# Splitting most gate and up weights in the prologue, turning the row maxima through DRAM, and asking for shared weight loads in an attention and GLU block

## The chip, the cores and the metric

The kernel runs on one core of a Trainium2 chip. The metric is the device time of one execution in microseconds (us). Three runs of the kernel before the change took 1661.74, 1663.04 and 1664.35 us, with a median of 1663.04. One more execution was taken with the hardware profiler; it took 1663.57 us, and its span from the first to the last instruction is 1661.8 us.

## What is computed

One transformer block over 2048 tokens of width 512, with a modulation vector computed from `c`. Attention has 32 query heads of width 16 and one shared key and value head; the feed-forward has a hidden width of 1792 and a sigmoid gate.

```
mod = silu(c) @ w_mod                      # six rows of 512: sa, ca, ga, sb, cb, gb
h = layernorm(x) * (1 + ca) + sa
q, k, v = h @ wq, h @ wk, h @ wv           # q: 32 heads x 16; k, v: one head x 16
p = softmax(q k^T / 4)                     # over all 2048 keys
x = x + ga * ((p v) @ wo)
h = layernorm(x) * (1 + cb) + sb
x = x + gb * ((sigmoid(h @ w_gate) * (h @ w_up)) @ w_down)
```

## The kernel before, in words

**Numbers as pairs.** Large products run in 16-bit floats, with every operand split into a high part and a low remainder, so that a product is three passes (high by high, high by low, low by high). The products for `p v` run in 32-bit floats.

**Units and steps.** Attention is cut into 32 units: 16 blocks of 128 queries (`QU`), each in two halves of 16 heads. A unit has 16 steps (`NKB`), one for 128 keys each, so the main loop (L1190) has 512 steps. A step has two half-steps. In each half-step, in the order that `ORDER` (L57) writes down, TensorE makes two `a` tiles (scores in one layout, bank `sa`, of which VectorE takes the row maximum into `mx`, L640), two `s` tiles (scores in the other layout, bank `st`, which ScalarE turns into `P` with an exponential, L678) and one `c` group (`P` times `V` into the bank `craw`, L691). The `a` tiles run 84 tiles (`A0`) ahead of the `s` tiles, since the maxima of a unit must be known before its first `s` tile. There are three `sa` banks and two `st` banks (L87). Matmuls are cut into tiles of 64 rows by 32 columns (`columns`, L152), so that the two halves of the array run different things at once: `a` and `s` on one half, `c` on the other.

**The way of the maxima.** When 64 maxima tiles of unit i are there (some five steps before the unit's first step), `max_end` (L652) reduces them with two VectorE instructions, `max_rows` (L659) turns them with two small TensorE matmuls through an `sa` bank, ScalarE copies and scales them twice, VectorE makes the low part, and four DMAs put two rows into each half of the unit's query tile `qp` (rows 48 and 49, 112 and 113). The first `s` tile of the unit reads these rows.

**The feed-forward as filling.** After each block of 128 queries its output projection and feed-forward (`ffn_block`, L868) are handed out in small pieces: `piece` (L1178) puts a few of its matmuls behind each half-step, at a rate that `pace` (L1141) works out from what is left. Pieces are `po` (output projection, group `wo`), `pgu` (gate and up), `pd` (down), and in the first three units `pq` (the queries that the prologue left). A group starts when its inputs are marked as issued a number of steps ago (`needs`: `EGAP` steps for the first block, `HGAP` for the others). The chain ahead of a block's `wo` is `unit_end`, `place`, `recip`, `recip2`, `recip3`, `finish` (L712 to L763): ScalarE evicts `craw` into `cs`, and five dependent steps of DMA, VectorE and GpSimd put the normalized rows into `a`. Behind `wo` come `norm` and `norm2` (L912, L918) on GpSimd with one VectorE statistic between, and a transposing DMA `h<-rows`. `defer(n, f)` means that f is written n steps later.

**The weights.** Gate and up weights, `wo` and the down weights are split into high and low in the main loop by 46 jobs (`weight_jobs`, L808). A job loads 128 by 512 numbers (`wst`), and three GpSimd instructions split them (L370 to L372); gate and up are then stored to DRAM (`wD`) and read again for each block as `gw` tiles. `WSTEPS` = 60 spreads the jobs over 60 steps. The first `gw` load is asked for when the last gate and up job has been stored.

**Queues.** TensorE, VectorE and ScalarE instructions and the DMAs of the main loop (`sp1`, issued by SyncE, SP) stay in written order. GpSimd (POOL) instructions of the main loop are placed by the framework's scheduler. Each queue runs in order, so a DMA that waits for its source holds up the DMAs behind it.

**Prologue.** `PLAN` (L38) is a list of tokens that fixes the order before the main loop: layer norm and transposes of the input (`S`, `N`, `T`, `H`, `E`, `L`), keys and values (`pk`, `KB`, `KL`, `pv`, `V`), the first queries (`q`, `QA`, `QL`), the modulation (`lm`, `pm`, `me`, `pr`, `m`), the first 84 maxima tiles (`a` a product, `x` its maximum), and the maxima chain of unit 0 (`mx`, `my`, `mz`).

Of the kernel before, what the change touches and what calls it, by code (L numbers as in the profile page):

```python
# [56 lines left out]
ORDER = "a0", "s0", "c", "a1", "s1"  # L57
# [5 lines left out]
SKIP = 9  # L63
GAP = 2
EGAP = 4
HGAP = 3
CHAIN = 24
QRATE = 1.5
MOST = 3
# [3 lines left out]
WSTEPS = 60  # L73
WLAST = 66
# [18 lines left out]
NGW = 4 * NPR + 2  # L93


@with_exitstack
def adaln_mqa_glu_kernel(
# [100 lines left out]
    class Couple:  # L198
# [3 lines left out]
        def part(self, n0, n1):  # L202
# [4 lines left out]
            for n in range(n0, n1):  # L207
# [3 lines left out]
                for j in (1 - side[0], side[0]):  # L211
                    g = self.gs[j ^ (n >= m)]
                    l_, r_, *cut = g.term(n % m, slice(64 * j, 64 * j + 64))
                    columns(cut[0](g.bank) if cut else g.bank, l_, r_, n == 0, n == 2 * m - 1)
# [15 lines left out]
    class Halves:  # L230
# [6 lines left out]
        def part(self, n0, n1):  # L237
# [4 lines left out]
            for n in range(n0, n1):  # L242
                for j in (1 - side[0], side[0]):
                    columns(self.banks[j], *self.term(n, slice(64 * j, 64 * j + 64)), n == 0, n == self.n - 1)
                if n in self.after:
                    self.after[n]()
# [36 lines left out]
    xall = pro.tile([P, NKB, D], F32, name="xall")  # L283
# [3 lines left out]
    def load_x(b):  # L287
        sp.dma_start(xall[:, 4 * b:4 * b + 4, :], x[b * QB:(b + 1) * QB, :].rearrange("(t p) d -> p t d", p=P))
# [15 lines left out]
    for t in range(4):  # L304
        sp.dma_start(xall[:, t, :], x[t * P:(t + 1) * P, :])
# [145 lines left out]
    def xs(b):  # L451
        return [xall[:, 4 * b + t, :] for t in range(4)]
# [150 lines left out]
    def load_q(i):  # L603
        b, o = units[i]
        qp = blanks.pop(0) if blanks else blank(pool)
        for j in range(2):
            src = qD[:, 2 * o * P:2 * (o + 1) * P, b * QU:(b + 1) * QU].rearrange("h (r j d) q -> j h d r q", j=2, d=DH)[j]
            for g, hl in ((0, 0), (1, 1), (2, 0)):
                spq().dma_start(qp[64 * j + 16 * g:64 * j + 16 * (g + 1)], src[hl])
        qps[i] = qp  # L610
# [13 lines left out]
    def spot(n):  # L624
        return n // 16, n % 2, n // 2 % 8

    def a_product(i, n):
# [3 lines left out]
        kc, j, r = spot(n)  # L631
# [4 lines left out]
        else:  # L636
            columns(sa, l_, r_, True, True)
        return i, n, sa

    def a_max(i, n, sa):  # L640
        kc, j, r = spot(n)
# [5 lines left out]
    def a_tile(i, n):  # L647
        a_max(*a_product(i, n))
# [3 lines left out]
    def max_end(i):  # L652
        m16 = wp.tile([64, 32], F32, tag="m16", name="m16", bufs=4)
        for u in range(2):
            dve.tensor_reduce(m16.rearrange("p (h u) -> p h u", u=2)[:, :, u], mxs[i][64 * u:64 * u + 64],
                              axis=AX.X, op=ALU.max)
        return lambda: max_rows(i, m16)

    def max_rows(i, m16):  # L659
        qp = get_q(i)  # L660
        pm = sbank("sa")
        pe.matmul(pm[:32, :64], m16, ident[:64, :64], start=True, stop=True)
        m32 = wp.tile([32, 64], F32, tag="m32", name="m32", bufs=4)
        act.activation(m32, pm[:32, :64], AF.Identity, scale=1.0 / SM)
        mh = wp.tile([32, 2, 64], F16, tag="mh", name="mh", bufs=4)
        act.activation(mh[:, 0], m32, AF.Identity)

        def low():
            dve.tensor_tensor(mh[:, 1], m32, mh[:, 0], op=ALU.subtract)
            for h in range(2):  # L670
                for j in range(2):
                    r = 64 * j + 48 + h
                    sp1.dma_start(qp[r:r + 1], mh[16 * j:16 * j + 16, h, :])

        return low
# [51 lines left out]
    def place(b, o, cs, lD, rD):  # L727
# [7 lines left out]
        defer(W1, lambda: recip(b, o, lD, rD))  # L735

    def recip(b, o, lD, rD):
# [11 lines left out]
        def recip3():  # L749
            for z in range(2):  # L750
                sp1.dma_start(raw[:, (2 + z) * QU:(3 + z) * QU], lD[1][8 * z:8 * z + 8].unsqueeze(1).to_broadcast([8, DH, QU]))
            defer(W3, lambda: finish(b, o, raw))

        defer(W2, recip2)
# [566 lines left out]
```

## Time and profile before

| what | us |
|---|---|
| median of three runs | 1663.04 |
| the profiled execution, whole | 1663.57 |
| its span, first to last instruction | 1661.8 |
| prologue, to the first eviction of an `st` bank | 114.8 |
| 32 units, first to last `st` eviction | 1471.0 |
| what follows | 76.0 |

The 1.8 us between the profiled execution's time and its span lie outside the instructions. The page gives for each engine its busy time; matmuls overlap, so a busy TensorE is not one at its peak. A view by stretches gives the busy time of each engine between two times; a unit shows in it as 64 evictions `P<-st`. A timeline gives the start of merged instructions in us from the span's start, then how long the row lasts; what stands in brackets is the idle time ahead of it and what ended it.

### The profile page before, as it was taken

The page shows a single profiled execution, that of the slowest core. Times are in us where ns is not written, and L with a number is a line of the kernel's source. Part 1 is how long each engine was busy: PE and PEld are TensorE (multiplying, and loading weights), DVE is VectorE, ACT ScalarE, POOL GpSimd, SP SyncE. Part 2 cuts the span into 40 slices and gives each one's busy share as a digit, 9 for nine tenths or more (in the row PEclk, how much of TensorE's full clock was granted, in tenths as well). Part 3 has the DMA queues.
Part 4 walks back from the last instruction along what each step waited for, and adds up shares of the span by engine and source line. Part 5 has one row for each costly group of instructions (what it writes and reads, how often), then busy time and mean ns, then how long its engine had stood idle before and what let it go on. Part 6 is the DMA issues. An engine that isn't in the chain of part 4 may idle for free.

```text
span 1661.8 us, 92905 instructions
## 1 busy us (share of the span) xinstructions
PE 1601.6 (96%) x41875; PEld 989.8 (60%) x41875; DVE 1440.8 (87%) x2410; ACT 1302.8 (78%) x2346; POOL 710.2 (43%) x864
## 2 busy tenths in 40 slices
PE   6899997989999999999999999999999999999998
PEld 3335553646666666666666666666666666666544
DVE  7689997879999999999999999999999999998031
ACT  5528886878888888888888888888888888888821
POOL 4353887461442525352534425262525344251510
PEclk9879998999999999999999999999999999999999
DMA  6232555550573535454462735463454537353653
GB/s 211 94 106 74 163 149 163 169 138 21 139 164 85 140 87 127 99 129 114 117 135 86 165 89 142 91 133 82 132 111 120 135 83 165 85 139 88 157 168 107
DMA packets 246681, 203.60 MB, mean 123 GB/s; under 512 B 125468, under 2 KB 177420, under 8 KB 246284
## 3 DMA queue, kind: packets, MB, share of 16 engines
q1 hardware_dynamic: 246284, 197.66, 46.3%
q8 instruction: 328, 5.37, 1.4%
q14 instruction: 69, 0.57, 0.1%
HBM read 159.97 MB, written 20.30 MB: 108 GB/s over the span
## 4 chain that ended last, share of the span: by engine, by line
PE 87%; ACT 4%; DVE 3%; POOL 2%; issue 2%; DMA 1%; SPq 0%; ACTq 0%; POOLq 0%; DVEq 0%
PE craw L143 23%; PE pgu L143 18%; PE sa L143 17%; PE st L143 10%; PE pd L143 8%; PE pq L143 3%; PE po L143 2%; DVE mx L143 2%; PE pd L257 2%; PE pgu L194 2%; ACT P L143 2%; ACT th L143 1%; PE pk L143 1%; DMA wm<-in_w_mod_dram 0%; PE pmod L143 0%
## 5 line engine op out<-in xcount | busy, mean ns | idle before, releaser
L143 DVE TENSOR_REDUCE mx<-sa 128x1 f32<-128x512 f32 x2048 | 1300.9, 683 | 96.7 <-PE sa L143 41.5
L143 ACT ACTIVATE P<-st 128x512 f32<-128x512 f32 x2048 | 1183.6, 597 | 230.2 <-PE st L143 162.6
L143 PE MATMUL craw<-P,V 64*32 64x512 f32 x8192 | 1100.5, 599 | 1.8 <-issue 1.3
L143 PE MATMUL st<-qp,kp 64*32 64x512 f16 x8192 | 844.3, 380 | 11.2 <-ACT P L143 9.7
L143 PE MATMUL sa<-kp,qp 64*32 64x512 f16 (+1 forms) x7940 | 840.7, 380 | 13.5 <-DVE mx L143 10.2
L143 PEld LDWEIGHTS <-kp 64*32 64x32 f16 x8192 | 323.9, 91 | 250.0 <-issue 83.0
L143 PE MATMUL pgu<-gw,h 64*32 64x512 f16 x9600 | 423.9, 377 | 9.3 <-DMA h<-rows 5.0
L143 PEld LDWEIGHTS <-qp 64*32 64x32 f16 (+1 forms) x7940 | 276.1, 92 | 146.1 <-issue 62.5
L143 PEld LDWEIGHTS <-h 64*32 64x32 f16 (+1 forms) x9792 | 209.2, 92 | 90.4 <-issue 28.1
L143 PEld LDWEIGHTS craw<-P,V 64*32 64x32 f32 x8192 | 195.6, 105 | 26.9 <-issue 13.2
L143 PE MATMUL pd<-wdh,g 64*32 64x512 f16 x2912 | 152.7, 376 | 2.4 <-issue 1.5
L967 POOL TENSOR_SCALAR th<-th 128x512 f32<-128x512 f32 (+1 forms) x57 | 32.3, 566 | 254.3 <-ACT th L143 243.6
L143 PEld LDWEIGHTS <-g 64*32 64x32 f16 x4368 | 94.7, 92 | 34.2 <-issue 8.0
L143 PE MATMUL pd<-wdl,g 64*32 64x512 f16 x1456 | 91.0, 376 | 0.0
L1020 POOL TENSOR_TENSOR o<-o,gb 128x512 f32<-128x512 f32 x13 | 16.7, 1282 | 166.1 <-ACT o L143 166.1
L600 POOL MEMSET qp<- 32x1024 f16 x60 | 56.6, 944 | 68.4 <-PE st L143 60.6
L968 POOL TENSOR_TENSOR th<-th,u 128x512 f32<-128x512 f32 (+1 forms) x57 | 65.3, 1146 | 4.8
L895 POOL TENSOR_TENSOR rows<-th,rows 128x512 f16<-128x512 f32 (+1 forms) x57 | 59.5, 1044 | 4.8
L143 PE MATMUL po<-woh,a 64*32 64x512 f16 x960 | 52.9, 377 | 1.9 <-ACT th L143 1.4
L143 PE MATMUL craw<-nought 64*32 64x1 f16 x329 | 53.7, 163 | 0.0
L143 PE MATMUL pq<-h,wdh 64*32 64x512 f16 (+1 forms) x688 | 51.9, 386 | 0.6 <-POOL h L143 0.4
L143 DVE COPY u<-pgu 128x512 f32<-128x512 f32 x43 | 29.3, 681 | 26.1 <-PE pgu L143 26.1
(163 smaller groups left out, 1139.8 us busy)
## 6 DMA issues: line engine op xcount, KB each, us to landing
gw<-wD SPq DMA_DIRECT2D x448, 256.0 KB
wD<-gw SPq DMA_DIRECT2D x28, 256.0 KB
wm<-in_w_mod_dram SPq DMA_DIRECT2D x6, 1024.0 KB
qp<-qD SPq DMA_DIRECT2D x192, 32.0 KB
qD<-q SPq DMA_DIRECT2D x16, 256.0 KB
xr<-in_A_x_dram SPq DMA_DIRECT2D x16, 256.0 KB
out_dram<-ot SPq DMA_DIRECT2D x16, 256.0 KB
rD<-cs SPq DMA_DIRECT2D x124, 32.0 KB
```

What stands on the lines that cost most here:

```text
L143: return (lambda *a, **k: keep(f_(*a, **k))) if pinned else f_
L194: pe.matmul(cut[0](self.bank) if cut else self.bank, l_, r_, start=(n == 0), stop=(n == self.n - 1))
L257: pe.matmul(self.bank, *self.term(n, slice(0, P)), start=(n == 0), stop=(n == self.n - 1))
L600: eng.memset(qp[j:j + 32], 0.0)
L895: pool.tensor_tensor(rows[:, n:2 * n], src, rows[:, :n], op=ALU.subtract)
L967: pool.tensor_scalar(th, th, 1.0, 1.0, op0=ALU.add, op1=ALU.mult)
L968: pool.tensor_tensor(th, th, u_, op=ALU.mult)
L1020: pool.tensor_tensor(o2, o2, mods[5], op=ALU.mult)
```

## The change

It has four parts.

1. **Prologue.** The gate and up weights of five of seven column blocks (`JCH` = 5: 20 jobs) are split in the prologue: ScalarE makes the high part and the scaled copy, GpSimd the low part, each job with one load and two stores by DMA (`jl`, `jb`). The input blocks `xall` become four separate buffers, and two of them are used again by these jobs. 26 jobs are left for the main loop, over 52 steps. `PLAN` is written anew: the query products of the second to fourth group stand later, and the first query tile is loaded in two parts (`la`, `lb`).
2. **First block.** `wo` of block 0 is due after 5 steps of its unit in place of 9, its chain `place` to `finish` has waits of 1 step in place of 2, 3 and 2, `EGAP` is 3 in place of 4, and queries left wait for an urgent group that is due within 7 steps. `last_end` waits 2 steps in place of 1 before ScalarE reads what GpSimd adds.
3. **Maxima.** The chain of the maxima has no matmul: one VectorE reduction, one ScalarE copy, a VectorE difference, a VectorE 32 by 32 transpose, one DMA to DRAM (`mD`) and two DMAs from there into `qp`.
4. **Order and weight loads.** `ORDER` is `s0 a0 c a1 s1`; `spot` gives two `a` tiles that follow each other the same query weights; the second of them, and every third product of a feed-forward group, is written as a matmul that uses weights loaded before (`held`).

```diff
-    'lw0 lw1 lx2 lx3 lw2 lw3 pm1 S00 S01 me1 S02 pr1 S03 ra0 rb0 m1 pm0 rc0 N00 N01 N02 me0 N03 pr0 S10 wh0 S11 wl0 '
+    'lw0 lx2 lx3 lw1 lw2 lw3 pm1 S00 S01 me1 S02 pr1 S03 ra0 rb0 m1 pm0 rc0 N00 N01 N02 me0 N03 pr0 S10 wh0 S11 wl0 '
...
-ORDER = "a0", "s0", "c", "a1", "s1"
+ORDER = "s0", "a0", "c", "a1", "s1"
-SKIP = 9
+SKIP, SKIP0 = 9, 5
-EGAP = 4
+EGAP = 3
+QWAIT = 7
-WSTEPS = 60
-WLAST = 66
+WSTEPS = 52
+WLAST = 52
+JCH = 5
...
-    def columns(dst, l_, r_, start, stop):
+    def columns(dst, l_, r_, start, stop, held=None):
         for c_ in range(0, P, 32):
-            pe.matmul(dst[c_:c_ + 32], l_[:, c_:c_ + 32], r_, start=start, stop=stop)
+            if held is None:
+                pe.matmul(dst[c_:c_ + 32], l_[:, c_:c_ + 32], r_, start=start, stop=stop)
+            else:
+                pe.add_instruction(mybir.InstMatmult(
+                    start_tensor_calc=start, stop_tensor_calc=stop, tile_size=(64, 32), tile_position=(held, c_), ldweights=False,
...
-    def spot(n):
-        return n // 16, n % 2, n // 2 % 8
+    def spot(i, n):
+        if i == 0:
+            return n // 16, n % 2, n // 2 % 8
+        return n // 32 * 2 + n // 2 % 2, n % 2, n // 4 % 8
...
     def max_end(i):
-        m16 = wp.tile([64, 32], F32, tag="m16", name="m16", bufs=4)
-        for u in range(2):
-            dve.tensor_reduce(m16.rearrange("p (h u) -> p h u", u=2)[:, :, u], mxs[i][64 * u:64 * u + 64],
-                              axis=AX.X, op=ALU.max)
...
+        dve.tensor_reduce(m, mxs[i], axis=AX.X, op=ALU.max)
+        return lambda: max_high(i, m, mm)
...
+        act.activation(mm[:, :16], m, AF.Identity, scale=1.0 / SM)
...
+        dve.scalar_tensor_tensor(mm[:, 16:], m, 1.0 / SM, mm[:, :16], op0=ALU.mult, op1=ALU.subtract)
+        dve.transpose(mt, mm)
...
+        sp1.dma_start(mD.rearrange("c (b q) -> b c q", b=4), mt)
+        return lambda: lambda: max_rows(i, mD)
...
+            sp1.dma_start(qp[r:r + 2].rearrange("h r q -> h (r q)"), mD.rearrange("(h j r) q -> j h (r q)", h=2, j=2)[j])
...
-        defer(W1, lambda: recip(b, o, lD, rD))
+        defer(W1 if b else 1, lambda: recip(b, o, lD, rD))
...
-                defer(1, go)
+                defer(2, go)
...
+    def job_beat():
+        k, beat[0] = beat[0], beat[0] + 1
+        if k < len(jobs):
+            w_ = wst["f"][:, k % 4]
+            hi, lo = (wst["h"][:, k % 4, e].rearrange("p k n -> p (k n)") for e in range(2))
+            act.activation(hi, w_, AF.Identity, scale=SW)
+            act.activation(w_, w_, AF.Identity, scale=SW)
+            pool1.tensor_tensor(lo, w_, hi, op=ALU.subtract)
+        if k >= 2:
+            job_store(k - 2)
+            if k + 2 < len(jobs):
+                job_load(k + 2)
...
-            first_.ready = i * NKB + SKIP
+            first_.ready = i * NKB + (SKIP if b > 1 else SKIP0)
```

The built program shows what becomes of part 4 on TensorE. In a half-step in the middle of the main loop (`sa` is an `a` tile, `st` an `s` tile, `craw` the `c` group; the rows left out repeat the pair of rows above them for the other three column tiles) there stood before:

```order
L143 LDWEIGHTS qp
L143 MATMUL sa<-kp,qp 32x512
...
L143 LDWEIGHTS kp
L143 MATMUL st<-qp,kp 32x512
...
L143 MATMUL craw<-P_22350,V 32x512
L143 MATMUL craw<-P_22368,V 32x512
```

And there stands now:

```order
L146 LDWEIGHTS qp
L146 MATMUL sa<-kp,qp 32x512
...
L146 MATMUL craw<-P_22217,V 32x512
L146 MATMUL craw<-P_22240,V 32x512
...
L146 LDWEIGHTS qp
L146 MATMUL sa<-kp,qp 32x512
...
L146 LDWEIGHTS kp
L146 MATMUL st<-qp,kp 32x512
```

The `c` group now lies between the two `a` tiles and no `s` tile does; but the second `a` tile, written as one without a load, has its LDWEIGHTS in the built program all the same. Counted over the whole program there are 33,430 of these rows where there were 33,423, so no weight load has gone.

On the SP queue, in unit 2 (steps 34 to 37), on the way of block 0 to its output projection (`lD`, `rD`, `lc`, `raw` are its stations; `qp<-qD` loads the queries of unit 4) there stood before:

```order
L143 DMA lD<-cs 8x1x128 x2
L143 DMA rD<-cs 16x4x128 x4
L143 DMA wst<-in_B_w_gate_dram 128x2x256
L143 DMA lc<-lD 128x16
L143 DMA wst<-in_B_w_up_dram 128x2x256
L143 DMA qp<-qD 16x8x128 x6
L143 DMA wD<-gw 512x1x256 x2
L143 DMA wst<-in_B_w_gate_dram 128x2x256
L143 DMA lD<-rc 128x16
L143 DMA raw<-rD 128x2x128
```

And now:

```order
L146 DMA lD<-cs 8x1x128 x2
L146 DMA rD<-cs 16x4x128 x4
L146 DMA gw<-wD 128x1024 x2
L146 DMA wst<-in_B_w_down_dram 128x512
L146 DMA lc<-lD 128x16
L146 DMA gw<-wD 128x1024 x2
L146 DMA lD<-rc 128x16
L146 DMA raw<-rD 128x2x128
L146 DMA gw<-wD 128x1024 x2
L146 DMA wst<-in_B_w_down_dram 128x512
L146 DMA qp<-qD 16x8x128 x6
L146 DMA raw<-lD 128x1x128 x2
```

The loads of `gw`, which stood in unit 3, now lie between the stations, and `raw<-lD` comes right behind the six loads of the query tile. A little further on the same queue, ahead of the start of unit 3 (steps 40 to 46), there stood before the rows of the maxima (`qp<-mh`) among loads and stores of weights:

```order
L143 DMA wD<-gw 512x1x256 x2
L143 DMA wst<-in_B_w_gate_dram 128x2x256
L143 DMA wst<-in_B_w_up_dram 128x2x256
L143 DMA qp<-mh 1x16x64 x4
L143 DMA wD<-gw 512x1x256 x2
```

And now:

```order
L146 DMA qD<-q_4459 128x2x512
L146 DMA gw<-wD 128x1024 x2
L146 DMA wst<-in_B_w_down_dram 128x512 x2
L146 DMA_TRANSPOSE h_4963<-rows 128x4x128 x2
L146 DMA mD<-mt 4x32x32
L146 DMA qp<-mD 2x1024 x2
```

The two transposing DMAs of block 0, which wait for GpSimd's `rows`, have come ahead of the two steps of the maxima of unit 3.

More of the change, by code (lines that the diff above doesn't have):

```diff
@@ L282, in adaln_mqa_glu_kernel @@
     cT = cp.tile([P, NDC], F32, name="cT")
-    xall = pro.tile([P, NKB, D], F32, name="xall")
+    xall = [pro.tile([P, 4, D], F32, tag="xb", name="xb", bufs=4) for _ in range(4)]
     wkv = cp.tile([P, 2, NDC, DH], F32, name="wkv")
@@ L451, in xs @@
     def xs(b):
-        return [xall[:, 4 * b + t, :] for t in range(4)]
+        return [xall[b][:, t, :] for t in range(4)]
     pts = {}
@@ L826, in gate_up @@
                          g_[:, :, m], g_[:, :, 2 + m], [2, 256], store if m == 1 else None)
-        for i in range(NCH):
+        for i in range(JCH, NCH):
             for kk in range(2):
@@ L1083, in adaln_mqa_glu_kernel @@
         stages[name](*[int(z) for z in tok[len(name):]])
-    assert not held and apos == A0
+    assert not held and apos == A0 and beat[0] == len(jobs) + 2
     first.clear()
@@ L1106, in adaln_mqa_glu_kernel @@
     early = [Couple(q_group(*z), q_group(*y)) for z, y in zip(qleft[::2], qleft[1::2])]
+    for g in early:
+        g.b = 0
     work, urgent = early, []
@@ L1137, in pick @@
         for z in range(min(2, len(work))):
+            if work[z].stage == "q" and urgent and s > urgent[0].ready - QWAIT:
+                return
             if ready(s, work[z]) and (z == 0 or "dn" in (work[0].stage, work[1].stage)):
@@ L1208, in adaln_mqa_glu_kernel @@
                 z[1]()
-            ready_rows, rows[:] = rows[:], [max_end(*z) for z in late]
             an = A0 + 4 * (s - kb % 2)
```

98 lines of the change are left out of this document (54 added, 44 removed), and 21 rows, old and new, of the table PLAN.

## The prediction

> **What bounds the kernel now.** I read the stretches first, then a half-step in the timeline, the groups, and the waits one by one. The stretches are the prologue (0 to 114.8 us, in two), units 0 and 1, unit 3, units 4 to 9, and units 10 to 31; unit 2 lies between 203.1 and 247.1.
>
> ```profile
> core 0: us, PE busy (x) PEld busy (x) DVE busy (x) ACT busy (x) POOL busy (x), PEclk, DMA share, GB/s
> 0.00:66.00 66.00, 48.22 (x246) 24.15 (x246) 46.80 (x104) 39.34 (x62) 31.29 (x55) 0.90 0.56 191
> 66.00:114.80 48.80, 44.87 (x301) 13.51 (x304) 40.17 (x68) 9.37 (x17) 21.36 (x26) 0.82 0.26 76
> 114.80:203.10 88.30, 85.58 (x2180) 47.28 (x2180) 81.86 (x136) 76.27 (x139) 49.21 (x62) 0.96 0.38 107
> ...
> 247.10:302.60 55.50, 46.44 (x1017) 23.56 (x1012) 42.65 (x72) 37.00 (x69) 41.09 (x51) 0.88 0.55 172
> 302.60:584.70 282.10, 273.17 (x7771) 175.73 (x7755) 260.88 (x433) 233.98 (x423) 121.57 (x146) 0.99 0.47 119
> 584.70:1585.80 1001.10, 991.47 (x28903) 649.82 (x28894) 907.50 (x1498) 858.55 (x1549) 405.91 (x478) 1.00 0.49 118
> ```
>
> TensorE is the bound wherever the filling is full. Units 10 to 31 take 1001.1/22 = 45.5 us each, 1.422 per half-step; units 0 and 1, with little filling, take 88.3/64 = 1.38. Unit 3 takes 55.5: ten too many. What a half-step holds is in the timeline of TensorE:
>
> ```profile
> 947.37 2.53 DVE L143 TENSOR_REDUCE mx<-sa 128x1 f32<-128x512 f32 x4
> 947.97 0.40 PE L143 MATMUL sa<-kp,qp 64*32 64x512 f16 x4
> 948.19 0.40 PE L143 MATMUL st<-qp,kp 64*32 64x512 f16 x4
> ...
> 948.62 0.40 PE L143 MATMUL st<-qp,kp 64*32 64x512 f16 x4
> 948.83 0.49 PE L143 MATMUL pd<-wdl,g 64*32 64x512 f16 x8
> ```
>
> A maximum's tile and an `s` tile start 0.215 us apart (two pairs in 0.43), weight loads included, and the terms of the feed-forward behind them too. Four tiles and two terms of the feed-forward make 6 x 0.215 = 1.29; the `c` group runs on the other half. VectorE needs 2.53/4 = 0.63 per maximum. ScalarE's price, and how often TensorE is empty because of the two, stand in the groups:
>
> ```profile
> L143 ACT ACTIVATE P<-st 128x512 f32<-128x512 f32 x2048 | 1183.6, 597 | 230.2 <-PE st L143 162.6 <-PE sa L143 8.3 <-PE pgu L143 2.3
> L143 PE MATMUL st<-qp,kp 64*32 64x512 f16 x8192 | 844.3, 380 | 11.2 <-ACT P L143 9.7 <-issue 1.2
> L143 PE MATMUL sa<-kp,qp 64*32 64x512 f16 x7856 | 813.1, 379 | 5.0 <-DVE mx L143 4.6
> ```
>
> The long stops are single ones:
>
> ```profile
> 263.53 0.61 PE L143 MATMUL sa<-kp,qp 64*32 64x512 f16 x4 [3.71 <-DVE mx L143]
> 285.63 0.63 PE L143 MATMUL pgu<-gw,h 64*32 64x512 f16 x8 [4.30 <-DMA h<-rows]
> 367.96 0.62 PE L143 MATMUL st<-qp,kp 64*32 64x512 f16 x4 [5.31 <-ACT P L143]
> ```
>
> The first two lie in unit 3. VectorE's wait behind the first is for GpSimd, which was splitting weights between two instructions of `norm`:
>
> ```profile
> 257.41 1.27 POOL L914 TENSOR_TENSOR xr<-t,xr 128x512 f32<-128x512 f32 x1
> ...
> 260.00 0.62 POOL L370 TENSOR_SCALAR wst<-wst 128x512 f32<-128x512 f32 x1
> ...
> 283.09 1.15 POOL L895 TENSOR_TENSOR rows<-t,rows 128x512 f16<-128x512 f32 x1
> ```
>
> **The change part by part**, against the profiled execution's 1663.57 us, which is 0.5 above the median of the runs.
>
> *Weight loads.* Not one goes (the count in the built program), and rows 0.215 apart show them hidden anyway: 0.
>
> *Prologue.* Twenty jobs add two ScalarE instructions and one GpSimd instruction each; nearest rows:
>
> ```profile
> L143 ACT ACTIVATE wdh<-wqs 128x512 f16<-128x512 f32 x4 | 2.5, 630 | 1.0 <-DMA wqs<-in_A_wq_dram 1.0
> L143 POOL TENSOR_TENSOR wdl<-wqs,wdh 128x512 f16<-128x512 f32 x3 | 3.5, 1155 | 3.7 <-ACT wqs L143 3.7
> ```
>
> ScalarE: 20 x 2 x 0.63 = 25.2 us on the 9.4 busy of 48.8. GpSimd: 20 x 1.16 = 23.2 on 21.4, 44.6 of 48.8. DMA: 256 KB in and 256 KB out per job, 10.5 MB; at the 191 GB/s that cost a share of 0.56 in the first 66 us that is 10.5/(0.191/0.56) = 31 us of the 48.8 x 0.74 = 36 free. VectorE, 40.2 of 48.8 and the bound there with its 84 maxima, gets nothing. So 0, with GpSimd's near-full stretch as the cover; if the jobs wait for each other, +6; if query products put later relieve it, -4.
>
> *Units 0 to 2, spacing.* Here ScalarE binds: 2 x 0.597 = 1.19 of 1.38. The `s` tiles stood 0.43 and 0.95 apart; `a0` between them makes it 0.65 and 0.73. I take a third of the 0.19 for 64 half-steps, -4 (-10 to +3).
>
> *Unit 2, block 0 comes early.* A new stop. SP's queue in unit 2 before:
>
> ```profile
> 208.16 1.17 SPq L143 DMA_DIRECT2D lD<-cs  x2
> 209.37 1.79 SPq L143 DMA_DIRECT2D rD<-cs  x4
> 211.21 0.43 SPq L143 DMA_DIRECT2D wst<-in_B_w_gate_dram  x1
> 211.75 1.27 SPq L143 DMA_DIRECT2D lc<-lD  x1
> 213.06 0.44 SPq L143 DMA_DIRECT2D wst<-in_B_w_up_dram  x1
> 213.54 3.90 SPq L143 DMA_DIRECT2D qp<-qD  x6
> ```
>
> Landing, the price of two `gw`, and GpSimd's share are in these, of unit 3:
>
> ```profile
> 285.76 1.33 SPq L143 DMA_DIRECT2D raw<-lD  x2
> ...
> 287.14 0.92 SPq L143 DMA_DIRECT2D gw<-wD  x2
> ```
>
> ```profile
> 288.90 0.73 POOL L760 TENSOR_TENSOR raw<-raw 128x256 f32<-128x256 f32 x1 [4.66 <-DMA raw<-lD]
> 289.72 0.41 POOL L761 TENSOR_SCALAR a<-raw 128x256 f16<-128x256 f32 x1
> ```
>
> Now, from the same 208.16: `lD` 1.17, `rD` 1.79, two `gw` 0.92, a load 0.44, `lc` 1.27 and two `gw` 0.92 end at 214.7. Then `lD<-rc` and `raw<-rD` (as long as a load and as `lc`'s shortest, some 0.4 each), two `gw`, a load, the six `qp<-qD` (3.90) and two `raw<-lD` (1.33): 222.1, or 223 if the reciprocal is waited for. GpSimd starts 288.90 - 287.09 = 1.8 us behind that and takes 0.73 + 0.41 for the high part of `a`: 225 to 226, with a low part of some 0.7 behind it. The group `wo` is due at step 38.5, at 203.1 + 6.5 x 2.75 = 221.0, and is urgent, so TensorE stops for 4 to 6 us. The `norm` steps that follow put a VectorE statistic behind GpSimd again, 1 to 2 us. I take +7 (+2 to +12).
>
> *Unit 3.* Both stops and the shortage of filling go: the feed-forward starts nine steps earlier, and unit 3 gets 504 of its matmuls where it had 224 (counted in the built program, as all such counts here). GpSimd's chain from 257.41 to 284.24, 26.8 us, held five splits of 0.62 + 0.62 + 1.16 = 2.4 us; in the changed order two stand there. What takes the place of the stops: `mD` for unit 3 stands on SP behind the transposes `h<-rows`, which wait for that chain. I take it 4 us late (0 to 7). So 55.5 becomes 45.2 + 4 = 49.2: -6.3.
>
> *Units 4 to 9.* 282.1 us; at 45.5 each they would take 273. Their filling falls from 3080 matmuls to 2784. Between units 0 and 1 (340 each, 44.15 us) and units 10 to 31 (551, 45.5) a matmul is worth 1.35/211 = 0.0064 us; at 464 each the six would take 6 x (45.5 - 87 x 0.0064) = 269.6, with all stops gone, the one of 5.31 first. I take -11 (-14 to -4).
>
> *Chain of the maxima.* Rows of the chain before:
>
> ```profile
> L143 DVE TENSOR_REDUCE m<-mx x64: 199/214/217, 101.7 to 1530.9; 64x16 f32<-64x64 f32 x64
> L143 PE MATMUL sa<-ident,m x64: 213/215/240, 103.4 to 1535.0; 64*32 64x64 f32 x64
> L143 ACT ACTIVATE m<-sa x32: 197/198/213, 103.7 to 1535.7; 32x64 f32<-32x64 f32 x32
> L143 ACT ACTIVATE mh<-m x32: 255/255/257, 103.9 to 1535.9; 32x64 f16<-32x64 f32 x32
> L143 DVE TENSOR_TENSOR mh<-m,mh x32: 212/595/1168, 104.2 to 1536.4; 32x64 f16<-32x64 f32 x32
> ```
>
> Gone per unit: two matmuls and an `sa` bank for their time, 0.25 of ScalarE. VectorE had 2 x 0.214 + 0.595 = 1.02 and gets one reduction (0.21), the difference (0.595) and a transpose, which no row shows: between 0.21, as a reduction of such size, and 0.6, as the difference; I take 0.21, since it has one input. That is 1.02 again. The Trainium skill, "VectorE: DVE Perf Modes", section "The three transpose paths", gives 0.311 us for 128x128 in 16 bits on VectorE; no run here shows it yet, and by it VectorE's part would be 1.12, 0.1 more in 31 units, 3 us. What goes is TensorE's place for one matmul, 0.215 or a little more with its bank, since the other may fall beside a `c` group: 31 x 0.23 = 7: -7 (-14 with both; +12 if the transpose costs 0.6 and VectorE binds, 31 x 0.39).
>
> *Order in the full half-steps.* Of TensorE's 9.7 us emptied by ScalarE, 5.3 is the stop at 367.96; the other 4.4 should go: -5. Half-steps are 1.422 against 1.29 of work, 0.13 x 896 = 118 us over 28 units; a sixth of it gone would be -20, and +10 is where VectorE begins to bind, the start of rival D. The tail has the same instructions: 0.
>
> Sum: 0 - 4 + 7 - 6.3 - 11 - 7 - 5 = -26.3; 1663.57 - 26.3 = 1637.3, 1637 after the 0.5 to the median.
>
> **The rivals.** (0.2%, 3.3 us, is about what a measurement of this kernel tells from no change.)
>
> *A, the maxima land late in every unit; slower.* They now need two DMAs one behind the other. The nearest pair of rows in the full part:
>
> ```profile
> 1063.15 0.34 SPq L143 DMA_DIRECT2D lD<-rc  x1
> ...
> 1064.96 0.66 SPq L143 DMA_DIRECT2D raw<-lD  x1
> ```
>
> From the end of one issue to its dependent's start 1063.49 to 1064.96, 1.47; in unit 2 `lD<-cs` to `lc<-lD` at most 211.75 - 209.33 = 2.42. So store 0.65, leg, two loads 1.3, leg: 4.9 to 6.8 us. From the transpose, three quarters into step 13 of 16, to the unit's first `s` tile are 2.25 x 2.84 = 6.4. If the legs take 2.4 each and SP is busy for 1 us more, each unit stops 1.5 us: 30 x 1.5 = 45, so 1637 + 45 = 1682. It decides from legs of about 2.2 on. Chance 0.13. The Trainium skill, "DMA: Bandwidth & Descriptors", section "Anatomy of one DMA — SWDGE (gpsimd) path", gives about 2.0 us fixed for a DMA, on GpSimd's path: legs of 4.0 in all and a chain of 5.9, 0.5 inside the limit, where the row of 1.47 leaves 1.5; the trace so far shows both sides of 2.0.
>
> *B, new stops eat the early gain.* The stop in unit 2 grows to 12, `mD` is 7 late, and the six units give 4: 1637 + 5 + 3 + 7 = 1652, and with the order at 0 some 1657; about 1655. Chance 0.17.
>
> *C, the spacing frees more.* -20 for the order and -10 in units 0 to 2 in place of -5 and -4: 1637 - 21 = 1616, 1612 with the chain at -11. For it: ScalarE has 0.11 us idle per tile ended by TensorE. Against: TensorE is seldom empty by ScalarE. Chance 0.15.
>
> *D, the `a` tiles bunch; slower.* `a0` and `a1` now stand with only `c`, which runs on the other half, between: 0.215 apart, then nothing for 1.2. VectorE, 907.5/704 = 1.29 per half-step of 1.422, must live on three banks. If it idles 0.17 per half-step for want of a tile, a half-step is 1.46: 0.04 x 896 = 36, so 1673. It decides where VectorE's queue runs empty, from 0.13 idle on. Chance 0.10.
>
> That the loads do go has no chance left by the built program.
>
> **How the numbers follow.** Main case 0.45 (1627 to 1648 from its terms), A 0.13, B 0.17, C 0.15, D 0.10. The likeliest gives 1637. The range reaches from below C's nearer end, 1610, to 1674, which holds B and D and leaves A out. Faster by over 0.2%: 0.45 + 0.15 + four fifths of B = 0.74. Slower: A less a little of it, and D with the last of A and B's tail, 0.21. Within: 0.05.
>
> **What would show it.** Right: evictions from 114.8 as before; a TensorE stop of 4 to 6 us near 221 with `po` waiting for GpSimd's `a`; unit 3 under 50 us; units 10 to 31 at 45.0 to 45.3. Wrong: a prologue that ends after 121; `st` waiting for the DMA of the maxima at each unit's start (A); `mx` with much more idle time ended by `sa` (D); a transpose over 0.6 us.

## The result, and the profile after

Over 18 runs of each, the changed kernel takes 1674.99 us (median; 1665.51 to 1679.13) and the kernel before 1659.63 (1654.18 to 1664.40). The ratio is 1.0088, with a 95% interval of 1.0072 to 1.0105: slower by some 15 us, where 26 less was forecast. The profiled execution of the changed kernel took 1675.08 us, with a span of 1673.3.

The view by stretches of the changed kernel, cut at the same places as that of before: prologue, units 0 and 1, unit 2, unit 3, units 4 to 9, units 10 to 31, tail.

```profile
core 0: us, PE busy (x) PEld busy (x) DVE busy (x) ACT busy (x) POOL busy (x), PEclk, DMA share, GB/s
0.00:140.20 140.20, 95.49 (x540) 38.13 (x544) 86.71 (x172) 72.00 (x118) 68.61 (x91) 0.81 0.59 181
140.20:227.70 87.50, 83.90 (x2176) 47.90 (x2176) 80.86 (x136) 74.66 (x137) 41.00 (x51) 0.96 0.27 77
227.70:284.70 57.00, 45.07 (x1155) 24.16 (x1147) 42.35 (x71) 37.66 (x70) 33.11 (x42) 0.94 0.43 131
284.70:329.10 44.40, 44.21 (x1299) 27.96 (x1291) 41.92 (x70) 38.27 (x71) 29.40 (x37) 1.00 0.57 170
329.10:601.80 272.70, 262.21 (x7465) 168.14 (x7450) 255.49 (x430) 227.44 (x415) 103.51 (x124) 0.99 0.40 100
601.80:1597.50 995.70, 981.14 (x28872) 651.18 (x28859) 894.01 (x1499) 843.67 (x1528) 409.42 (x482) 1.00 0.48 119
1597.50:1673.30 75.80, 69.18 (x375) 32.29 (x367) 20.40 (x35) 9.71 (x18) 0.57 (x1) 1.00 0.42 139
```

The first two columns, each stretch and its length, hold the answer. Against before: prologue +25.4, units 0 and 1 -0.8, unit 2 +13.0, unit 3 -11.1, units 4 to 9 -9.4, units 10 to 31 -5.4, tail -0.2. The gains in the units are there; the prologue takes them all, and unit 2 takes part.

In the prologue the timelines show one long stop. VectorE and TensorE first:

```profile
108.83 0.22 DVE L146 TENSOR_REDUCE m<-mx 128x16 f32<-128x64 f32 x1
108.97 1.36 DVE L146 TENSOR_REDUCE mx<-sa 128x1 f32<-128x512 f32 x2
128.61 1.18 DVE L146 SCALAR_TENSOR_TENSOR mm<-m,mm 128x16 f16<-128x16 f32 x1 [18.28 <-ACT mm L146]
```

```profile
130.66 8.95 PE L146 MATMUL sa<-kp,qp 64*128 64x512 f16 x15 [19.51 <-DVE mx L146]
```

VectorE has reduced the maxima of unit 0 at 108.83, takes two more tiles, and stands 18.28 us at the difference `mm`, which needs ScalarE's `mm`. The maxima of the last tiles stand behind it, so the `sa` banks stay full and TensorE stops for 19.51. Where ScalarE is in this time:

```profile
107.02 1.29 ACT L146 ACTIVATE xb<-xb 128x512 f16<-128x512 f32 x2 [4.01 <-DMA xb<-in_B_w_gate_dram]
111.83 1.29 ACT L146 ACTIVATE xb<-xb 128x512 f16<-128x512 f32 x2 [3.52 <-DMA xb<-in_B_w_up_dram]
...
127.19 1.29 ACT L146 ACTIVATE xb<-xb 128x512 f16<-128x512 f32 x2 [3.66 <-DMA xb<-in_B_w_up_dram]
128.38 0.20 ACT L146 ACTIVATE mm<-m 128x16 f16<-128x16 f32 x1
```

Every `xb<-xb` pair is a weight job; ScalarE takes them in order and waits for their loads. `mm<-m`, 0.20 us long, comes behind the last one. From 73.62, where the first job begins on ScalarE, to 128.48, where the last one ends, are 54.9 us: 2.74 per job, of which ScalarE works 1.29. The loads are late on SP:

```profile
97.71 0.57 SPq L146 DMA_DIRECT2D xb<-in_B_w_up_dram  x1
102.10 0.37 SPq L591 DMA_DIRECT2D qD<-q  x1
...
118.27 0.57 SPq L146 DMA_DIRECT2D xb<-in_B_w_gate_dram  x1
122.16 0.37 SPq L591 DMA_DIRECT2D qD<-q  x1
...
131.06 0.65 SPq L146 DMA_DIRECT2D mD<-mt  x1
```

Between 98.28 and 102.10, and between 118.84 and 122.16, SP issues nothing: the store of queries `qD<-q` waits there for GpSimd's `q<-q,q`, which ends at 102.07 and 122.14, and the next loads stand behind it.

Unit 2 of the kernel before, for comparison:

```profile
203.10:247.10 44.00, 42.71 (x1136) 23.43 (x1118) 40.39 (x69) 38.58 (x71) 39.19 (x50) 1.00 0.54 152
```

Now TensorE stops there four times for more than 1 us, at the reciprocal's place, at the output projection, at the layer norm's statistic, and at the first `s` tile of unit 3:

```profile
243.64 0.62 PE L146 MATMUL sa<-kp,qp 64*32 64x512 f16 x4 [3.36 <-DVE mx L146]
```

```profile
253.77 0.62 PE L146 MATMUL po<-woh,a 64*32 64x512 f16 x8 [3.42 <-POOL a L774]
```

```profile
268.07 0.40 PE L146 MATMUL sa<-kp,qp 64*32 64x512 f16 x4 [2.26 <-DVE mx L146]
```

```profile
284.18 0.40 PE L146 MATMUL st<-qp,kp 64*32 64x512 f16 x4 [1.75 <-DMA qp<-mD]
```

The four make 10.8 of the 13.0. TensorE's busy time, with nearly as many rows, is 2.4 longer; the granted clock is 0.94 where it was 1.00. The second, third and fourth stop stood in the prediction. The first did not; VectorE's timeline tells what it is:

```profile
242.79 0.25 DVE L146 RECIPROCAL rc<-lc 128x16 f32<-128x16 f32 x1 [4.18 <-DMA lc<-lD]
```

`lc<-lD` is issued at 238.07 and lands 4.7 us later, with loads of `gw` ahead of it and behind it; `recip`, now one step after `place`, meets it on VectorE, and the maxima queue up behind.

The maxima's chain on VectorE, over all units (shortest, median and longest in ns, then the first and last start):

```profile
L146 DVE SCALAR_TENSOR_TENSOR mm<-m,mm x32: 161/177/1175, 128.6 to 1548.3; 128x16 f16<-128x16 f32 x32
L146 DVE STREAM_TRANSPOSE mt<-mm x32: 210/211/214, 129.8 to 1548.5; 128x32 f16<-128x32 f16 x32
```

### The profile page after: what moved, and what is told of

Same layout as the page of the kernel before. It is cut to its first block, busy times and chain, and to the rows that moved or that the text cites. A ratio compares the mean times of both kernels' runs of the same rounds, so it can differ in the third digit from the quotient of the medians.

```text
span 1673.3 us, 92934 instructions
## 1 busy us (share of the span) xinstructions
PE 1581.2 (94%) x41818; PEld 989.8 (59%) x41818; DVE 1421.7 (85%) x2410; ACT 1303.4 (78%) x2354; POOL 685.6 (41%) x824
## 3 DMA queue, kind: packets, MB, share of 16 engines
q1 hardware_dynamic: 247084, 197.92, 44.6%
## 4 chain that ended last, share of the span: by engine, by line
PE 79%; DMA 6%; DVE 5%; ACT 5%; issue 2%; SPq 1%; POOL 1%; ACTq 0%; POOLq 0%; DVEq 0%
PE craw L146 22%; PE pgu L146 17%; PE sa L146 13%; PE st L146 12%; PE pd L146 7%; DVE mx L146 3%; ACT P L146 3%; PE po L146 2%; PE pd L266 2%; PE pq L146 2%; PE pgu L203 2%; DMA qp<-mD 1%; DMA xb<-in_B_w_up_dram 1%; SPq L146 1%; DMA mD<-mt 1%
## 5 line engine op out<-in xcount | busy, mean ns | idle before, releaser
L146 ACT ACTIVATE P<-st 128x512 f32<-128x512 f32 x2048 | 1166.7, 597 | 239.0 <-PE st L146 180.3
L146 PE MATMUL sa<-kp,qp 64*32 64x512 f16 (+1 forms) x7940 | 658.8, 380 | 35.9 <-DVE mx L146 33.5
L146 PEld LDWEIGHTS <-kp 64*32 64x32 f16 x8192 | 331.9, 91 | 279.4 <-issue 106.4
L146 PEld LDWEIGHTS <-qp 64*32 64x32 f16 (+1 forms) x7940 | 259.5, 93 | 134.9 <-issue 73.2
L146 PEld LDWEIGHTS <-h 64*32 64x32 f16 (+1 forms) x9792 | 214.9, 92 | 84.2 <-issue 27.7
L146 PEld LDWEIGHTS craw<-P,V 64*32 64x32 f32 x8192 | 242.9, 105 | 23.0 <-issue 8.5
L609 POOL MEMSET qp<- 32x1024 f16 x60 | 56.7, 944 | 55.3 <-PE st L146 53.0
L146 PE MATMUL po<-woh,a 64*32 64x512 f16 x960 | 59.4, 386 | 6.6 <-POOL a L774 6.6
```

Of the source, the lines that this page charges most:

```text
L146: return (lambda *a, **k: keep(f_(*a, **k))) if pinned else f_
L609: eng.memset(qp[j:j + 32], 0.0)
```

## The experiments

All profiled executions, cut at the evictions of `st` (us); the rows below refer to this table:

| kernel | prologue | units 0, 1 | unit 2 | unit 3 | units 4 to 9 | units 10 to 31 |
|---|---|---|---|---|---|---|
| before | 114.8 | 88.3 | 44.0 | 55.5 | 282.1 | 1001.1 |
| changed | 140.2 | 87.5 | 57.0 | 44.4 | 272.7 | 995.7 |
| copy of unit 0's maxima on VectorE | 137.1 | 88.8 | 56.5 | 44.6 | 269.4 | 998.3 |
| loads ahead of stores | 136.5 | 87.8 | 55.6 | 44.8 | 268.0 | 999.4 |
| jobs four beats earlier | 139.0 | 87.7 | 57.4 | 45.1 | 267.2 | 1003.2 |
| eight stages | 125.9 | 87.7 | 58.2 | 44.4 | 269.7 | 995.3 |
| 12 jobs | 121.2 | 87.4 | 59.9 | 46.3 | 268.1 | 1000.0 |
| first block as before | 141.3 | 88.0 | 44.1 | 46.5 | 269.1 | 997.0 |
| no jobs, first block as before | 118.9 | 89.4 | 42.9 | 53.7 | 274.5 | 997.4 |
| 12 jobs, first block as before | 121.6 | 88.3 | 44.2 | 43.6 | 271.7 | 1002.8 |
| the same in the old plan | 111.0 | 88.7 | 44.3 | 43.2 | 270.9 | 996.3 |
| 20 jobs, the same, old plan | 132.8 | 87.8 | 43.1 | 47.1 | 272.3 | 997.5 |
| before, with the order | 110.1 | 86.9 | 43.6 | 55.3 | 280.5 | 997.9 |
| before, with the maxima | 111.6 | 88.2 | 44.1 | 57.0 | 281.3 | 994.6 |
| before, with both | 109.7 | 87.2 | 43.6 | 56.1 | 278.6 | 993.2 |

With the old plan and no jobs the prologue lay between 109.7 and 114.8 in four kernels, profiled once each. The order alone changes nothing ahead of the main loop, and that kernel's prologue still ended 4.7 us earlier than that of the kernel before. So up to 5 us of a single prologue carry no argument.

**The copy of unit 0's maxima on VectorE.**

```diff
+        if i == 0:
+            dve.tensor_scalar(mm[:, :16], m, 1.0 / SM, 0.0, op0=ALU.mult, op1=ALU.add)
+        else:
-        act.activation(mm[:, :16], m, AF.Identity, scale=1.0 / SM)
+            act.activation(mm[:, :16], m, AF.Identity, scale=1.0 / SM)
```

> Theory (the jobs' queue): in the prologue of the changed kernel VectorE stands 18.3 us at the difference of unit 0's maxima, because ScalarE's copy before it lies behind the weight jobs, which wait for their loads. Here VectorE makes that copy for unit 0, so its stop of 18.3 and TensorE's of 19.5 must go. But the store of the maxima lies behind the jobs' stores on SP until 131, so the first unit can start only at about 135 to 136 where it started at 140.2: a gain of 4 to 5 us. Rival (only the copy is late): the first eviction comes at about 122, 18 us gained. Rival (DMA or GpSimd set the end whatever waits): 140.

One run, 1672.25 us. The prologue ends at 137.1. TensorE's timeline, and SP's:

```profile
136.47 0.62 PE L146 MATMUL st<-qp,kp 64*32 64x512 f16 x4 [15.42 <-DMA qp<-mD]
```

```profile
125.54 6.39 SPq L146 DMA_DIRECT2D wD<-xb  x8
132.03 0.65 SPq L146 DMA_DIRECT2D mD<-mt  x1
134.12 0.60 SPq L146 DMA_DIRECT2D qp<-mD  x2
```

VectorE's stop is gone, and TensorE stops all the same, 15.42 us, one place further on: `mD` waits on SP behind the jobs' last eight stores. The stop at `mm` was where the jobs were met first, not the only place; some 3 of the 25 us come back, no more.

**No jobs, and the first block's steps as before.**

```diff
-JCH = 5
+JCH = 0
-WSTEPS = 52
-WLAST = 52
+WSTEPS = 60
+WLAST = 66
-SKIP, SKIP0 = 9, 5
-EGAP = 3
-QWAIT = 7
+SKIP, SKIP0 = 9, 9
+EGAP = 4
+QWAIT = -99
```

`jl` and every `jb` leave the plan, the jobs of `wo` stand in the main loop where they stood before, and the waits in `place` and `recip` are W1, W2 and W3 for all blocks.

> No weight jobs in the prologue and the first block's steps as before the change; new plan, maxima and order stay. Theory: the prologue ends at 115 to 118 us, units 2 to 9 are as before the change (44, 55, 282), units 10 to 31 stay at 996: about 1655 to 1660, 15 to 20 under the changed kernel and 0 to 6 under the kernel before. Rival (the new plan or the four input buffers make the prologue long): it still ends after 125.

1657.13 us against 1662.27; ratio 0.9975 (0.9948 to 1.0003). The prologue ends at 118.9: without the jobs 21 of the 25 us are gone. The gain in unit 3 is gone too (53.7). This run changes two things; with the first block's steps as before and all 20 jobs, below, the gain stays, so it comes with the prologue's jobs.

**Twelve jobs.**

```diff
-JCH = 5
+JCH = 3
```

The last eight `jb` leave the plan.

> Twelve jobs in the prologue in place of 20, 34 in the main loop. Theory: at 2.74 us a job the last one is done near 107, ahead of the maxima's chain, so the stop of 19.5 goes and the prologue ends at 119 to 123; units 2 and 3 lose a little since eight jobs more lie in them: 1655 to 1660 in all. Rival (the stop has another cause than the jobs behind which the chain lies): the prologue stays over 130.

1661.12 us; ratio 1.0004 (0.9979 to 1.0029). The prologue ends at 121.2, as expected. Unit 2 grows to 59.9, with these two stops of TensorE in it:

```profile
234.67 0.63 PE L146 MATMUL po<-woh,a 64*32 64x512 f16 x8 [7.61 <-POOL a L774]
```

```profile
267.76 0.61 PE L146 MATMUL st<-qp,kp 64*32 64x512 f16 x4 [7.27 <-DMA qp<-mD]
```

More weights are left to split beside the first block. Its short steps meet them: with the steps of before beside the same twelve jobs, below, both stops are gone.

**Loads ahead of stores in each beat.**

```diff
         if k >= 2:
-            job_store(k - 2)
             if k + 2 < len(jobs):
                 job_load(k + 2)
+            job_store(k - 2)
```

> Each beat asks for the next load ahead of the two stores on SP. If the jobs' pace of 2.74 us is set by waiting in SP's order (a load stands behind stores that wait for GpSimd), the jobs end 4 to 10 us earlier and the first eviction comes at 130 to 136. If it is set by what the DMA engines move (share 0.70 to 0.78 in this stretch), the pace stays within 0.1 of 2.74 and the prologue within 2 us of 140.

One run, 1669.77 us; prologue 136.5. The pace goes from 2.74 to 2.59 us a job (72.90 to 124.73 on ScalarE); in the two other runs that leave the jobs as they are, the copy on VectorE and the first block as before, it is 2.75. Between the two expectations: the order on SP counts, but this is not the whole of it.

**The first block's steps as before, all else changed.** `SKIP0`, `EGAP`, `QWAIT` and the waits are those of the run without jobs; `JCH` stays 5, with the 20 jobs in the plan.

> The first block's steps as before the change (due after 9 steps, waits of 2, 3 and 2, no holding back of queries), the 20 jobs of the prologue and all else stay. Theory: the 13 us that unit 2 lost are the price of the first block's short steps, so unit 2 falls from 57.0 to 44 or 45; unit 3 keeps part of its gain, since fewer weights are left to split, at 46 to 51 in place of 44.4. The sum of units 2 to 9 falls by 4 to 10 from 374.0 (the profiled execution of the changed kernel). Rival (unit 2 is slow because the loads of the feed-forward's weights, now ready early, crowd the DMA): unit 2 stays over 52.

One run, 1663.46 us. Two stretches of it, units 2 and 3:

```profile
229.20:273.40 44.20, 41.94 (x1139) 24.22 (x1124) 40.09 (x69) 37.85 (x72) 24.75 (x32) 1.00 0.55 174
273.40:319.80 46.40, 41.08 (x1010) 22.18 (x1005) 41.35 (x72) 36.66 (x68) 31.81 (x41) 0.96 0.25 70
```

Unit 2 is 44.2 again and unit 3 stays at 46.4, although TensorE has only 1010 matmul rows in it, as few as before the change (1017) and not the 1299 of the changed kernel. So the short unit 3 is no work of filling brought forward. One of its two long stops has gone, the one of 4.30 at `h<-rows`. GpSimd's chain up to there, which ran from 257.41 to 284.24 (26.8 us), now takes 19.4, with two splits of weights between its steps in place of five:

```profile
281.30 1.27 POOL L927 TENSOR_TENSOR xr<-t,xr 128x512 f32<-128x512 f32 x1
...
299.56 1.16 POOL L908 TENSOR_TENSOR rows<-t,rows 128x512 f16<-128x512 f32 x1
```

The other one, at the layer norm's statistic, has stayed:

```profile
289.93 0.61 PE L146 MATMUL sa<-kp,qp 64*32 64x512 f16 x4 [4.03 <-DVE mx L146]
```

Of the 9.1 us that unit 3 is shorter, 3.7 are idle time of TensorE; the other 5.4 are its busy time, 41.08 in place of 46.44 with as many rows, at a granted clock of 0.96 in place of 0.88. In the kernel before, the clock stood at 0.50 behind each of the two stops. The view by stretches shows it behind the second, and full again behind that:

```profile
285.63:292.20 6.57, 5.89 (x96) 2.47 (x104) 2.66 (x6) 1.93 (x4) 1.80 (x3) 0.50 0.70 214
292.20:302.60 10.40, 10.40 (x314) 6.37 (x302) 10.12 (x16) 8.75 (x17) 7.98 (x10) 1.00 0.51 171
```

These are 16 rows of matmuls per busy us and 30, so this stop of 4.30 us cost more than its own length.

Units 2 to 9 take 359.7 where the changed kernel takes 374.1. The first block's shorter steps cost 14 us there and gain nothing in the units behind.

**The kernel before with the new order alone**, and **with the new maxima alone**: `ORDER` of the change; and `max_end` to `max_rows` of the change with its main loop around them, and three more `my` in the plan for the longer chain of unit 0.

> The kernel before with the new order of tiles alone. Theory (the order frees TensorE): units 10 to 31 fall from 1001 by 3 to 8, units 0 and 1 by 0 to 2. Rival (the gain of 5.4 there is the maxima's): within 2 of 1001. Rival D of the prediction (bunched a tiles starve VectorE): above 1010.

> The kernel before with the new way of the maxima alone. Theory (two matmuls, a bank and part of ScalarE's and VectorE's work go in each unit): units 10 to 31 fall from 1001 by 2 to 6. Rival (the gain there is the order's): within 2 of 1001. Rival A of the prediction (the maxima land late): above 1010.

Order: 1652.00 us against 1661.08, ratio 0.9950 (0.9928 to 0.9972). Maxima: 1649.64, ratio 0.9927 (0.9900 to 0.9955). Each is a gain by itself. In single profiles units 10 to 31 give 3.2 and 6.5 of it; the same stretch lies between 993 and 1003 in all kernels of the table with both parts, so how much belongs to which unit is not to be read from one profile.

**Both in the kernel before.**

> The kernel before with both the new order and the new way of the maxima. Alone they took 0.5% and 0.73% (medians 9 and 11 us). Theory (they are separate): 1640 to 1645. Rival (both give the same thing, fewer waits between the tiles of a half-step): 1649 to 1652, as either alone.

1646.11 us against 1660.56, ratio 0.9911 (0.9881 to 0.9942). 14 us, where the two alone took 9 and 11: the intervals overlap with that of the maxima alone, so whether they add up in full stays open.

**Twelve jobs with the first block's steps as before.**

> Twelve jobs in the prologue and the first block's steps as before the change. Theory: the prologue ends near 121 as with twelve jobs alone, and the stops of 7.6 (output projection) and 7.3 (maxima of unit 3) go, so unit 2 falls from 59.9 to 44 or 45, and unit 3 lies at 48 to 54 in place of 46.3: 1648 to 1656 in all. Rival (the stops only move into unit 3): unit 3 above 56 and 1660 or more.

1642.21 us, ratio 0.9908 (0.9875 to 0.9941). Unit 2 is 44.2 and unit 3 is 43.6, better than expected. Units 2 to 9 take 359.5 against 374.3 with twelve jobs and the short steps: 15 us, about the 14 that it was with twenty.

**The same with the plan of the kernel before**, one job after every third maximum, the maxima's chain of unit 0 in single steps behind its last ones.

> Twelve jobs and the first block's steps of before, as in the run with those two, but with the plan of the kernel before, into which the jobs are set one after every third maximum. Theory (the new plan itself costs some 5 us of prologue, since the run without jobs ended it at 118.9 and plans of before at 110 to 115; twelve jobs fit beside it): the prologue ends at 112 to 118 in place of 121.6, and the whole is 1634 to 1641. Rival (twelve jobs cost what they cost, wherever they stand): 121 or more, 1642 to 1648.

1637.34 us, ratio 0.9851 (0.9821 to 0.9880): faster than both kernels. The prologue ends at 111.0, so twelve jobs fit into it for nothing. The new plan cost 10.6 us of prologue beside them in the two profiled executions (121.6 with it) and 5 us in the medians. Against the kernel before with order and maxima (1646.11) it is 9 us less, and unit 3 takes 43.2 in place of 56.1.

**Twenty jobs, four beats earlier.**

```diff
-    ... L33 bl jl x pk32 x pk33 V1 a KB3 a a x jb a ...
+    ... L33 bl jl x jb pk32 jb x jb pk33 V1 a jb KB3 a a x jb a ...
```

> The changed kernel with its 20 jobs, four beats put earlier, so that ScalarE begins them near 62 us in place of 73.6, in a stretch where the DMA share was 0.01; nothing else changed. Theory (the jobs' pace of 2.6 to 2.8 us and their place in ScalarE's and SP's queues ahead of the maxima set the end): they end near 118 in place of 129, the stop falls from 19.5 to about 9 and the prologue ends at 128 to 132. Rival (the stop is of the last jobs' DMAs, whenever the first ones start): 138 or more.

One run, 1677.17 us; prologue 139.0. My theory fails here. ScalarE does its first four jobs at 71.08, not near 62, and then:

```profile
84.16 1.29 ACT L146 ACTIVATE xb<-xb 128x512 f16<-128x512 f32 x2 [7.57 <-DMA xb<-in_B_w_gate_dram]
...
125.95 1.29 ACT L146 ACTIVATE xb<-xb 128x512 f16<-128x512 f32 x2 [1.18 <-DMA xb<-in_B_w_up_dram]
```

The fifth job waits 7.57 us for its load, since SP's first store comes only at 79.70 (78.81 in the changed kernel). GpSimd's low parts, which the stores need, begin no earlier, behind its `memset`s:

```profile
74.50 3.94 POOL L609 MEMSET qp<- 32x1024 f16 x4
78.52 4.49 POOL L146 TENSOR_TENSOR xb<-xb 128x512 f16<-128x512 f32 x4
```

The last job ends at 127.2, where it ended at 128.5. The stop itself did fall, from 19.51 to 9.17:

```profile
129.42 8.95 PE L146 MATMUL sa<-kp,qp 64*128 64x512 f16 x15 [9.17 <-DVE mx L146]
```

But the maxima of unit 0 were complete only at 117.86, where they had been at 108.83, so most of these 10 us were lost ahead of the stop. So it is not the place of the jobs in the plan that sets their end, but their own loop, from the first store on.

**Eight stages.** The other two input buffers are used too, and loads run six jobs ahead.

```diff
-            wst["f"] = pro.tile([P, 4, D], F32, tag="xb", name="xb", bufs=4)
-            wst["h"] = pro.tile([P, 4, 2, 2, 256], F16, tag="xb", name="xb", bufs=4)
+            wst["f"] = [pro.tile([P, 4, D], F32, tag="xb", name="xb", bufs=4) for _ in range(2)]
+            wst["h"] = [pro.tile([P, 4, 2, 2, 256], F16, tag="xb", name="xb", bufs=4) for _ in range(2)]
...
-            if k + 2 < len(jobs):
-                job_load(k + 2)
+            if k + 6 < len(jobs):
+                job_load(k + 6)
```

> The changed kernel with eight stages for the jobs in place of four (the other two input buffers are used again as well), and loads asked for six jobs ahead in place of two. If the jobs' pace of 2.5 to 2.7 us comes from waiting for a load that was asked for late (a loop of load, ScalarE, GpSimd, store over four stages), the pace falls to the 1.9 us that SP takes to issue a job's three DMAs, the last job ends near 115 to 120 in place of 129, and the first eviction comes at 126 to 132. If the DMA engines are the limit (share 0.70 to 0.78), the pace stays above 2.4 and the eviction at 136 to 141.

One run, 1658.94 us, prologue 125.9. ScalarE's jobs run from 72.91 to 113.92, 2.05 a job; TensorE's stop is down to 5.76:

```profile
115.11 8.95 PE L146 MATMUL sa<-kp,qp 64*128 64x512 f16 x15 [5.76 <-DVE mx L146]
```

The DMA engines moved more in the stretch with most of the jobs than they had:

```profile
80.00:100.00 20.00, 18.51 (x120) 6.18 (x119) 13.99 (x23) 19.26 (x36) 16.01 (x15) 0.94 0.85 240
```

So the bandwidth was not the limit at 0.78 and 0.70, the shares of the changed kernel from 80 to 100 and from 100 to 120 us. With four stages a load is asked for only two jobs ahead, behind stores that wait for GpSimd and, on SP, behind the store of the queries. The number of stages and how far ahead the loads run were changed together, so how much belongs to which stays open.

**Twenty jobs in the plan of before**, first block as before, one job after every second maximum.

> Twenty jobs set into the plan of the kernel before, one after every second maximum, first block's steps as before. Theory (twelve jobs fit and twenty do not, in any plan, because from their first store near 78 on twenty jobs take 49 us): the prologue ends at 126 to 136. Rival (it was the new plan that made twenty jobs late): 118 or less, and 1640 or less in all.

One run, 1657.98 us, prologue 132.8. TensorE's two stops:

```profile
106.93 0.58 PE L146 MATMUL sa<-kp,qp 64*128 64x512 f16 x1 [6.36 <-DMA qp<-qD]
...
123.22 1.77 PE L146 MATMUL sa<-kp,qp 64*128 64x512 f16 x3 [13.12 <-DVE mx L146]
```

Twenty jobs over four stages are late in this plan also; the first stop shows what else they hold up on SP, the loads of the query tile of unit 1: SP issues them at 103.77, behind stores and loads of jobs and a store of queries.

## Why the prediction was wrong

**The step that failed** is "So 0, with GpSimd's near-full stretch as the cover; if the jobs wait for each other, +6." The prologue grew by 25.4, and a prologue that ends after 121 was the prediction's own sign of being wrong. I added up busy time, and all of it fits: the eight stages brought 14 us back with the same work, so busy time was not what set the 140. What I had put at 0 to 6 is the time that one job takes through load, ScalarE, GpSimd and store over four stages: 2.74 us a job, 55 us for twenty. Left out altogether was that in-order queues put the maxima of unit 0 behind the last job twice, on ScalarE (`mm`) and on SP (`mD`). "VectorE gets nothing" was true of its work, and it stood 18.28 us. The sum that was not made is the pace of that loop times twenty jobs, and its end set beside the maxima's chain. Whether the rows of before alone would have given a pace of 2.74 was not tried.

From the -26.3 of the forecast to the +11.5 between the two profiled executions are 37.8 us: 25.4 in the prologue, 6.0 in unit 2, 3.2 in units 0 and 1, 6.4 for maxima and order, counted in units 10 to 31 and what follows, 1.6 in units 4 to 9, less 4.8 in unit 3. So all that lies behind the prologue gained 14, not 26. In units 0 and 1, where -4 was forecast for the spacing, -0.8 came; the order alone gave -1.4 there in a single profile.

**Unit 2**: +7 forecast, +13.0 measured. The stops at the output projection (3.42, forecast 4 to 6) and at the statistic (2.26, forecast 1 to 2) were right in kind. The forecast followed SP to 0.2 us up to the second pair of `gw` loads (6.5 us forecast, 6.7 measured). Then SP waited for the reciprocal from 239.47 to 243.07, 3.6 us where 1 was allowed, since `lc` landed 4.7 us after its issue, among the `gw` loads, where the forecast's legs were 1.5 to 2.4. That VectorE and with it TensorE would stop for it (3.36) was left out. The rest of the excess is the late maxima of unit 3 (1.75), counted there in the forecast, and the lower clock.

**Unit 3 and units 4 to 9**: -6.3 and -11 forecast, -11.1 and -9.4 measured. The late maxima of unit 3 (4 forecast) were 1.75 and lie in unit 2's count; without them unit 3 was forecast at 45.2 and came at 44.4. That the size is so near is in part luck, since the reason is half wrong. With the first block's steps undone unit 3 stays at 46.5, so what shortens it is GpSimd's lighter load and, with it, the clock, which the forecast did not have, and not the nine steps. The nine steps moved the stop at the statistic into unit 2.

**Maxima and order**: -7 and -9 forecast, -11 and -9 measured in the kernel before, 14 together where 16 was forecast; in the changed kernel units 10 to 31 give 5.4, where their share of the two terms is about 9 (7 x 22/31 and 5 x 22/28). The transpose takes 0.211, as taken. The Trainium skill, "VectorE: DVE Perf Modes", section "The three transpose paths", gives 0.311 us for four times the width; the 0.211 here does not contradict it. The difference takes 0.177 where I used 0.595, which may be why the maxima gained more than I gave them; no run separates it. That no weight load went is borne out: the changed kernel's profile has 41,818 loads for 41,818 matmuls.

**The rivals.** A stayed at its edge. In six units, the first of them unit 7, the two legs lie in the chain that ended last; in one:

```profile
821.38 2.07 DMA mD<-mt
823.77 3.46 DMA qp<-mD
```

The legs run from the issue, so they hold the 0.65 and 1.3 that I added to them: from 821.38 to 827.23 are 5.9 us of the 6.4 there were. The waits of TensorE and of its weight loads from unit 4 on, in the view of waits (us in total, times, longest):

```profile
PEld L146 <- DMA qp<-mD: 5.2, 10, 0.9
PE st L146 <- DMA qp<-mD: 1.2, 4, 0.4
```

So the room is used up in some units, for a few us in all, not for 45. The Trainium skill, "DMA: Bandwidth & Descriptors", section "Anatomy of one DMA — SWDGE (gpsimd) path", gives about 2.0 us fixed for a DMA on GpSimd's path; these DMAs are issued by SP. The first leg (2.07) lies near that figure, the second (3.46) does not. D did not come either: order alone is faster. C, the spacing frees more, did not come: the order gave 9. For C the forecast read ScalarE's idle time as 0.11 us per tile ended by TensorE; that is all its idle time, and what TensorE ended is 0.08 (162.6 and 8.3 over 2048). B, new stops that eat the gain, had unit 2 right (12 forecast, 13.0 measured), but not the late `mD` of unit 3 and not the six units behind. No rival had the prologue.

## What to carry to other kernels

A stage with idle engines takes extra work for nothing only if the extra work's own chain is short enough: count its jobs times the pace at which its buffers let them through, here 2.74 us over four stages and 2.05 over eight, and not only its busy time. On each in-order queue, ask which small instruction of the critical chain stands behind the last of the new jobs. Ask also what a stop costs behind its end: in unit 3 of the kernel before the granted clock was 0.50 behind stops of 3.71 and 4.30 us. And undo a change part by part: here the order, the maxima and the first twelve jobs gained, and the first block's steps, the new plan and eight jobs more cost more than that.

## What was not expected of the hardware

The same plan, in two kernels that differ only behind it, ended at 114.8 and at 110.1 us. The view by stretches, 40 to 60 us, shows the clock that TensorE was granted, first of the kernel before, then of it with the new order:

```profile
40.00:60.00 20.00, 17.35 (x70) 7.61 (x68) 12.29 (x21) 12.85 (x20) 8.67 (x8) 0.75 0.56 207
```

```profile
40.00:60.00 20.00, 17.72 (x81) 7.75 (x79) 14.70 (x25) 15.35 (x24) 9.40 (x9) 0.87 0.56 208
```

At 0.75 it did 70 rows of matmuls, at 0.87 81 in the same time. Why the clock differed, and whether it makes the whole difference, was not tried. The difference on VectorE with one 32-bit and one 16-bit input took 0.177 us on 128x16 numbers, where the one before took 0.595 on 32x64; the forms differ in more than one way, and why was not tried.
